# Gated mix of attention and a gated linear unit: two head groups' projections as 2x2 blocks with seven products, and five early head steps

## The chip, the cores and the metric

The kernel runs on one core of a Trainium2 chip. The metric is the time of one execution in microseconds; the figure given for a version is the median of its runs.

## The reference

One sequence of 2048 tokens, 512 wide. An attention with 32 heads of 16 and a gated linear unit with 1792 hidden channels are mixed by a gate per token:

```python
qkv = (x @ wqkv).reshape(B, S, 3, H, Dh)          # B, S, H, Dh = 1, 2048, 32, 16
p = softmax(einsum("bhqd,bhkd->bhqk", q, k) * Dh ** -0.5)
a = einsum("bhqk,bhkd->bhqd", p, v).reshape(B, S, D) @ wo
b = (sigmoid(x @ w_gate) * (x @ w_up)) @ w_down   # 512 -> 1792 -> 512
g = sigmoid((x * gate_w).sum(-1, keepdims=True))
out = g * a + (1 - g) * b
```

## The kernel before

**Precision.** Nearly every matrix product is made of high and low parts of its operands (f32r tiles): high by high, high by low and low by high, so each product of two 128-deep blocks is three matmuls. A `Sum` is such a product gathered in one PSUM bank; its matmuls are issued as halves of 64 rows (`Sum.half`, L161), the lower and the upper half of the array by turns.

**The steady loop.** Attention runs as 256 periods (`for k in range(NPER)`, L840), 16 for each of 16 pairs of heads. The string `STEADY` (L831) writes out the order of one period: the maxima's matmuls of a later stretch (L284, reduced by VectorE at L286), the score matmuls (L648, exponentials on ScalarE at L650), 12 filling halves, marked `d0` and `d1`, and then the 16 value matmuls (L781). The instructions of TensorE, VectorE, ScalarE and GpSimd (POOL) stay in the order written. SP, which issues nearly all DMAs, is not written in order: the scheduler places them, and SP then issues them strictly one after another. The last ten periods use `LAST`, with six halves.

**The filling.** The generator `filling()` hands out Sums. Jobs before, in order: the query and key projections of head groups 1, 2 and 3 (`qk`, 8 Sums of 24 halves each, periods k 0 to 47; group 0 is done ahead of the loop); then gate and up, whose 14 column blocks are taken in pairs as 2x2 blocks with seven products in place of eight, as Strassen and Winograd do: `far` (7 jobs, 4 products each), `side` (14 jobs of 4) and `chain` (14 jobs of 8), all of 12 halves, one product per period, up to k 243. In them x itself has to be replaced by sums and differences of its quarters (`mixed_x`, through `t_d` in memory); products are evicted by ScalarE (`out_of`), added by POOL (`plus`, L514) and stored to `gu_d` (L516). After them comes `heads`: for the first `EARLY` of eight steps u of the output projection, head groups 0 and 1 are summed in the loop (`first_heads_load`, `first_heads_split`) and kept in `hp_d`.

**Beside it.** The maxima of each half pair are split by POOL (`put_max`, L295; the cast at L311), stored in `max_d` (L304) and read back by four DMAs (L308) into the row of `qs` that the scores use. The logits of the gate are 16 VectorE instructions (L768) at k 78 to 125. The softmax denominators are turned into reciprocals by `denominators` (L756).

**The tail.** After the loop come 28 chunks of the down projection (L966, 24 matmuls each), and between them the eight steps `heads_out(u)`. A step below `EARLY` takes only head groups 2 and 3 and adds what `hp_d` holds:

```python
ks = range(2 if u < EARLY else 0, KT)
product(o, [((hl[0][:, n, cols], hl[1][:, n, cols]), (wohl[:, 0, k, :], wohl[:, 1, k, :]))
            for n, k in enumerate(ks)])
```

Each step has two output tiles; `product` is L148 in the profile.

## Time and profile before

| | before |
|---|---|
| median of 3 runs | 1695.69 us (1694.86 to 1696.26) |
| profiled execution | 1694.23 us, span 1692.5 us |
| TensorE busy | 1685.8 us, 100% of the span, granted clock 1.0 |
| VectorE, ScalarE, POOL busy | 1446.7, 1357.4, 880.7 us (85%, 80%, 52%) |
| chain that ended last | TensorE 96% |
| DMA | 223.51 MB, mean 132 GB/s |
| memory read, written | 131.33 MB, 89.92 MB |

The span runs from the first to the last instruction of the profiled execution; 1.73 us of that execution's time lie outside it. A line such as L308 is a line of the kernel before. PE is TensorE's matmuls, PEld its weight loads, DVE VectorE, ACT ScalarE, SPq the issue of a DMA on SP. The chain is the work that ended last, followed back from the last instruction to what released each piece. The profile is of one execution, and all durations below are its own.

### The profile page before, as it was taken

The page shows a single profiled execution, that of the slowest core. Times are in us where ns is not written, and L with a number is a line of the kernel's source. Part 1 is how long each engine was busy: PE and PEld are TensorE (multiplying, and loading weights), DVE is VectorE, ACT ScalarE, POOL GpSimd, SP SyncE. Part 2 cuts the span into 40 slices and gives each one's busy share as a digit, 9 for nine tenths or more (in the row PEclk, how much of TensorE's full clock was granted, in tenths as well). Part 3 has the DMA queues.
Part 4 walks back from the last instruction along what each step waited for, and adds up shares of the span by engine and source line. Part 5 has one row for each costly group of instructions (what it writes and reads, how often), then busy time and mean ns, then how long its engine had stood idle before and what let it go on. Part 6 is the DMA issues. An engine that isn't in the chain of part 4 may idle for free.

```text
span 1692.5 us, 34518 instructions
## 1 busy us (share of the span) xinstructions
PE 1685.8 (100%) x12509; PEld 1032.5 (61%) x12509; DVE 1446.7 (85%) x2333; ACT 1357.4 (80%) x2643; POOL 880.7 (52%) x862
## 2 busy tenths in 40 slices
PE   9999999999999999999999999999999999999999
PEld 7755555555555555555555555555555555568887
DVE  6988888888889989999888888889988888887643
ACT  4188888888898989888888989889898988984321
POOL 1033343447664555554666667676666667643110
PEclk9999999999999999999999999999999999999999
DMA  7412324254755352534625353535353434478762
GB/s 235 109 45 65 83 64 96 64 127 153 200 171 136 109 120 92 118 114 106 193 98 136 108 144 108 139 108 135 108 126 108 127 120 132 142 234 280 266 195 71
DMA packets 126922, 223.51 MB, mean 132 GB/s; under 512 B 23520, under 2 KB 33504, under 8 KB 123872
## 3 DMA queue, kind: packets, MB, share of 16 engines
q1 hardware_dynamic: 126752, 221.31, 44.9%
q8 instruction: 98, 1.61, 0.4%
q14 instruction: 72, 0.59, 0.1%
HBM read 131.33 MB, written 89.92 MB: 131 GB/s over the span
## 4 chain that ended last, share of the span: by engine, by line
PE 96%; DMA 1%; DVE 1%; POOL 1%; issue 0%; SPq 0%; ACT 0%; POOLq 0%; DVEq 0%
PE dn L161 30%; PE sm L781 27%; PE sm L284 12%; PE st L648 7%; PE sm L966 5%; PE sm L648 5%; PE st L284 2%; PE dn L966 2%; PE st L161 2%; PE st L966 2%; PE st L148 1%; PE st L612 1%; PE sm L148 1%; DVE stat L286 1%; DMA gul<-gu_d 1%
## 5 line engine op out<-in xcount | busy, mean ns | idle before, releaser
L286 DVE TENSOR_REDUCE stat<-sm 128x1 f32<-128x512 f32 x1310 | 848.5, 683 | 150.8 <-PE sm L648 129.6
L650 ACT ACTIVATE p<-st 128x512 f32<-128x512 f32 x1020 | 617.7, 652 | 1.4 <-PE st L648 0.8
L650 ACT ACTIVATE p<-sm 128x512 f32<-128x512 f32 x1026 | 608.8, 630 | 0.9 <-PE sm L648 0.9
L284 PE MATMUL sm<-ks,qs 48*128 48x512 f32 x1310 | 516.4, 435 | 0.3 <-DVE stat L286 0.3
L286 DVE TENSOR_REDUCE stat<-st 128x1 f32<-128x512 f32 x738 | 482.1, 681 | 0.1
L781 PE MATMUL sm<-p,v 128*17 128x512 f32 x4032 | 482.1, 595 | 0.0
L648 PE MATMUL sm<-qs,ks 64*128 64x512 f32 x1026 | 426.9, 419 | 0.3 <-DMA qs<-max_d 0.3
L648 PE MATMUL st<-qs,ks 64*128 64x512 f32 x1020 | 426.9, 419 | 0.2 <-DVE stat L286 0.2
L284 PEld LDWEIGHTS sm<-ks,qs 48*128 48x128 f32 x1310 | 233.9, 184 | 290.9 <-DVE stat L286 208.6
L798 POOL TENSOR_TENSOR sum<-sum,part 128x512 f32<-128x512 f32 x224 | 288.9, 1290 | 181.2 <-PE sm L648 169.1
L284 PE MATMUL st<-ks,qs 48*128 48x512 f32 x738 | 291.3, 395 | 0.0
L786 ACT ACTIVATE part<-sm 128x512 f32<-128x512 f32 x215 | 128.7, 599 | 133.0 <-issue 106.8
L781 PEld LDWEIGHTS sm<-p,v 128*17 128x17 f32 x4032 | 93.6, 96 | 227.2 <-issue 156.7
L648 PEld LDWEIGHTS st<-qs,ks 64*128 64x128 f32 x1020 | 187.7, 184 | 30.2 <-issue 3.4
L648 PEld LDWEIGHTS sm<-qs,ks 64*128 64x128 f32 x1026 | 189.1, 185 | 9.5 <-issue 4.3
L514 POOL TENSOR_TENSOR chain<-chain,chain 128x512 f32<-128x512 f32 x84 | 108.5, 1291 | 114.6 <-PE sm L648 112.1
L514 POOL TENSOR_TENSOR had<-chain,had 128x512 f32<-128x512 f32 x84 | 108.1, 1287 | 59.6 <-PE sm L648 43.0
L284 PEld LDWEIGHTS st<-ks,qs 48*128 48x128 f32 x738 | 137.8, 187 | 1.0 <-ACT v L631 0.3
L514 POOL TENSOR_TENSOR side<-side,side 128x512 f32<-128x512 f32 x28 | 36.1, 1291 | 92.7 <-PE sm L648 87.1
L576 ACT ACTIVATE chain<-dn 128x512 f32<-128x512 f32 x112 | 77.8, 694 | 0.0
L103 POOL TENSOR_TENSOR ol<-ot,oh 128x1024 fp32r<-128x1024 f32 (+1 forms) x8 | 16.4, 2054 | 101.9 <-ACT oh L100 101.9
L311 POOL CAST mhl<-mt 128x32 fp32r<-128x32 f32 x32 | 7.4, 233 | 102.7 <-DVE mt L292 102.7
(837 smaller groups left out, 3205.3 us busy)
## 6 DMA issues: line engine op xcount, KB each, us to landing
gul<-gu_d SPq DMA_DIRECT2D x56, 512.0 KB
had<-gu_d SPq DMA_DIRECT2D x84, 256.0 KB
gu_d<-had SPq DMA_DIRECT2D x84, 256.0 KB
gu_d<-side SPq DMA_DIRECT2D x56, 256.0 KB
qs<-q_d SPq DMA_DIRECT2D x90, 128.0 KB
ks<-k_d SPq DMA_DIRECT2D x90, 128.0 KB
pv_d<-sum SPq DMA_DIRECT2D x32, 256.0 KB
gu_d<-far SPq DMA_DIRECT2D x28, 256.0 KB
```

The source lines that it names most:

```text
L148: pe.matmul(o, a, b, start=(i == 0), stop=(i == len(ops) - 1))
L161: mm = pe.matmul(self.o, a[rows], b[rows], start=(self.n == 0), stop=(self.n == 2 * len(self.ops) - 1))
L284: pe.matmul(t, qs[r:r + KM, qt * P:(qt + 1) * P], ks[r:r + KM, g * 512:(g + 1) * 512], start=True, stop=True)
L286: dve.tensor_reduce(stat[half][:, b, qt % 8, g:g + 1], t, axis=AX.X, op=ALU.max)
L514: pool.tensor_tensor(to, u, w, ALU.add)
L576: leave = lambda e, o: act.activation(e, o, AF.Copy)
L648: pe.matmul(o, ks[r:r + KR, (kt + a) * P:(kt + a + 1) * P], qs[r:r + KR, q0:q0 + 512], start=True, stop=True)
L650: act.activation(pt[:, 2 * a + c, :], o, AF.Exp, scale=DH ** -0.5)
L781: pe.matmul(o[32 * c:32 * c + VW, :], v[:, 2 * k % 16 + a, h * VW:(h + 1) * VW], pts[c // 2][:, 2 * a + c % 2, :], start=(a == 0), stop=(a ...
L786: act.activation(e, o, AF.Copy)
L798: pool.tensor_tensor(s, s, e, ALU.add)
L966: pe.matmul(down[t], a, b, start=(f == 0 and m == 0), stop=(f == NF - 2 and m == 5))
```

## The change

`EARLY` becomes 5: steps u=3 and u=4, too, get the sums of head groups 0 and 1 in the loop, so `heads` has 10 Sums and not 6. The query and key projections of head groups 2 and 3 leave the `qk` jobs. They become an eighth `far` job and a `side` and a `chain` job each for queries (m=2) and keys (m=3), with groups 2 and 3 as the two column blocks. The jobs now run: `qk` 1 (k 0 to 15), eight `far` (16 to 47), `side` and `chain` of queries and keys (48 to 71), then `side` and `chain` of gate and up (72 to 239), then `heads`. The side job of the keys replaces quarters of x as that of gate and up does; for the side jobs that follow, `kept_x` stores these quarters beforehand in two more planes of `t_d` (8 DMAs of 512 KB), and the chain job of the keys fetches them back with `mixed_x`. The finished projections lie in `s_d` as f32; later, at k 75 to 122, they are fetched, split into high and low by POOL and stored to `q_d` and `k_d` (`split_load`, `split_sum`). The logits move three periods earlier, and the reciprocals of the first denominators are spread over twice as many pieces.

```diff
-EARLY = 3
+EARLY = 5
...
     pv_d = dram.tile([2, NPAIR, P, 512], F32, name="pv_d")
     hp_d = dram.tile([2 * EARLY, P, D], F32, name="hp_d")
-    t_d = dram.tile([3, 2, 2, 2, P, 512], F32, name="t_d")
+    t_d = dram.tile([5, 2, 2, 2, P, 512], F32, name="t_d")
+    s_d = dram.tile([2, 2, P, S], F32, name="s_d")
     max_d = dram.tile([2 * NPAIR, 4, 32, 2, 32], F32, name="max_d")
...
+    def kept_x(n, c, k0, cx):
+        cols = slice(cx * 512, (cx + 1) * 512)
+        for a, xs in enumerate((xh, xl)):
+            sp.dma_start(t_d[n, a, c].rearrange("k p s -> p k s"), xs[:, k0:k0 + 2, cols].bitcast(F32))
+
     def mixed_x(n, c, k0, cx):
 
         cols = slice(cx * 512, (cx + 1) * 512)
...
     def filling():
         pairs = [(m, i) for i in range(HF) for m in range(2)]
-        jobs = ([("qk", n) for n in range(1, D // P)] + [("far", i) for i in range(HF)]
-                + [("side", n) for n in pairs] + [("chain", n) for n in pairs] + [("heads", 0), ("down", 0)])
+        qk = [(2, 0), (3, 0)]
+        jobs = [("qk", 1)] + [("far", i) for i in range(HF + 1)]
+        for ns in (qk, pairs):
+            jobs += [("side", n) for n in ns] + [("chain", n) for n in ns]
+        jobs += [("heads", 0), ("down", 0)]
         gu_w = (w_gate, w_up)
+
+        def beside(m, i):
+            return i + HF if m < 2 else i + 1
 
         def raws(kind, n):
             if kind == "qk":
...
                 both = []
                 for m in range(2):
-                    sp.dma_start(raw[:, 2:], gu_w[m][n][:, 2:])
+                    sp.dma_start(raw[:, 2:], gu_w[m][n][:, 2:] if n < HF else wqk[2, 1, :, m])
                     both.append(raw)
                 return both
...
             if kind == "heads":
             m, i = n
+            if m >= 2:
+                return [raw_weights(wqk[f, :, :, m - 2].rearrange("b p k f -> p b k f"), [P, KT, P],
+                                    f"{kind}{m}_{f}") for f in (2, 3)]
             return [raw_cols(gu_w[m], i + a, f"{kind}{m}_{i + a}") for a in (0, HF)]
...
             return e
 
         def place(m, f, c):
-            return gu_d[m, f, :, c * 512:(c + 1) * 512]
+            to = gu_d[m, f] if m < 2 else s_d[m - 2, f]
+            return to[:, c * 512:(c + 1) * 512]
 
...
                     for c in range(2):
                         run = Sum(bankd(), quarter(ws[m], 2, c))
                         yield run
-                        sp.dma_start(place(m, n, c), out_of(run, f"far{m}{n}_{c}"))
+                        sp.dma_start(place(m, n, c) if n < HF else place(2 + m, 0, c), out_of(run, f"far{m}{n}_{c}"))
             elif kind == "side":
                 m, i = n
                 for c in range(2):
                     for a in range(2):
                         run = Sum(bankd(), quarter(ws[a], 2 * a, c + 2))
                         yield run
-                        if n == pairs[-1]:
+                        if n in (qk[-1], pairs[-1]):
                             mixed_x(1 + a, c, 2 * a, c + 2)
                         e = out_of(run, f"side{m}{i}_{c}{a}")
                         if a == 0:
                             first = e
-                            sp.dma_start(place(m, i + HF, c + 2), e)
+                            sp.dma_start(place(m, beside(m, i), c + 2), e)
                         else:
                             plus(e, e, first, place(m, i, c + 2))
             elif kind == "heads":
...
             else:
                 m, i = n
                 for c in range(2):
-                    to = [place(m, i, c), place(m, i, c + 2), place(m, i + HF, c + 2), place(m, i + HF, c)]
+                    i2 = beside(m, i)
+                    to = [place(m, i, c), place(m, i, c + 2), place(m, i2, c + 2), place(m, i2, c)]
...
                         run = Sum(bankd(), quarter(ws[a], k0, cx))
                         yield run
+                        if n == qk[-1] and a >= 2:
+                            mixed_x(1 + a, c, 2 * a - 4, c + 2)
                         e = out_of(run, f"chain{m}{i}_{c}{a}")
                         if a in (1, 2):
                             plus(e, e, first)
...
         def first_heads(u):
 
-            ks, q0 = slice(2 * (u // 2), 2 * (u // 2) + 2), (u % 2) * 256
+            ks, q0 = slice(u // 2 % 2 * 2, u // 2 % 2 * 2 + 2), (u % 2) * 256
             for at in (0, 2):
                 for xs in (xh, xl):
                     yield xs[:, ks, at * 512 + q0:at * 512 + q0 + 256]
...
                         mix_x(u // 2, u % 2)
                 if job == ("chain", pairs[-1]):
                     if at == 4:
-                        for u in range(EARLY):
+                        for u in range(4):
                             first_heads_load(u)
                     if at in (6, 7):
                         first_heads_split(at - 6)
-                if kind == "heads" and at == 2:
-                    first_heads_split(2)
+                if kind == "heads" and at in (2, 4, 6):
+                    if at == 2:
+                        first_heads_load(4)
+                    first_heads_split(at // 2 + 1)
                 if at == ask[kind][0]:
                     coming = raws(*nxt)
                 if at == ask[kind][1]:
...
             while end in later:
                 later.pop(0)[1]()
             ws = new
-            if kind == "far" and n == HF - 1:
+            if kind == "far" and n == HF:
                 flush(slow)
                 for c in range(2):
                     mixed_x(0, c, 2, c)
+                for c in range(2):
+                    kept_x(3, c, 0, c + 2)
+                    kept_x(4, c, 2, c + 2)
         wd.extend(ws)
...
 
+    split_in = {}
+
+    def split_load(r):
+        f, t, c = r // 8, r // 4 % 2, r % 4
+        e = split_in[r] = keep.tile([P, 2, 512], F32R, name=f"sq{r}", tag="ev", bufs=2)
+        sp.dma_start(e[:, 0, :].bitcast(F32), s_d[t, f, :, c * 512:(c + 1) * 512])
+
+    def split_sum(r):
+        f, t, c = r // 8, r // 4 % 2, r % 4
+        e = split_in.pop(r)
+
+        def store():
+            for a in range(2):
+                sp.dma_start((q_d, k_d)[t][a, (2 + f) * P:(3 + f) * P, c * 512:(c + 1) * 512],
+                             e[:, 1 - a, :].bitcast(F32))
+        split_later(e[:, 1, :], e[:, 0, :], e[:, 0, :].bitcast(F32), store)
+
...
 
-    dens = [denominators(0, 0, 32, 8), denominators(0, 32, 64, 2), denominators(1, 0, 64, 2)]
+    dens = [chain(denominators(0, 0, 32, 8), denominators(1, 0, 32, 8)), denominators(0, 32, 64, 2),
+            denominators(1, 32, 64, 2)]
...
-        if 78 <= k < 126:
-            t, r = divmod(k - 78, 6)
-            if r == 0:
+        if 75 <= k < 123:
+            t, r = divmod(k - 75, 6)
+            if r in (0, 3):
+                split_load(2 * t + r // 3)
+            if r in (1, 4):
+                split_sum(2 * t + r // 3)
+            if r == 1:
                 logit_load(2 * t)
             if r in (3, 4):
                 logits(2 * t, r - 3)
...
-        if 192 <= k < 202:
+        if 192 <= k < 212:
             next(dens[0], None)
         if k == NPER - 6:
             next(dens[1])
```

In the instruction order, names are tiles with the number of their buffer or of their use. The lines of the changed file are shifted: L149 is `product` (L148 before), L305 and L309 are the store and the loads of the maxima (L304 and L308), L378 and L379 the loads of heads and reciprocals (L372 and L373), L535 the store of an added sum (L516), L797 the store of split projections.

On TensorE, in the tail, step u=3 stands before chunk 15 of the down projection. `oh3` and `ol3` are the high and low parts of the heads, `wohl` the output weights, `sm0` and `st0` the two output tiles. Before, from the first matmul with `ol3` on:

```order
L148 MATMUL sm0_69<-wohl_18125,ol3_18599 128x512
L148 MATMUL sm0_69<-wohl_18125,oh3_18598 128x512 x2
L148 MATMUL sm0_69<-wohl_18125,ol3_18599 128x512
L148 MATMUL sm0_69<-wohl_18125,oh3_18598 128x512 x2
L148 MATMUL sm0_69<-wohl_18125,ol3_18599 128x512
L148 MATMUL sm0_69<-wohl_18125,oh3_18598 128x512 x2
L148 MATMUL sm0_69<-wohl_18125,ol3_18599 128x512
L148 MATMUL st0_65<-wohl_18125,oh3_18598 128x512 x2
L148 MATMUL st0_65<-wohl_18125,ol3_18599 128x512
```

After:

```order
L149 MATMUL sm0_69<-wohl_18348,ol3_18822 128x512
L149 MATMUL sm0_69<-wohl_18348,oh3_18821 128x512 x2
L149 MATMUL sm0_69<-wohl_18348,ol3_18822 128x512
L149 MATMUL st0_65<-wohl_18348,oh3_18821 128x512 x2
L149 MATMUL st0_65<-wohl_18348,ol3_18822 128x512
L149 MATMUL st0_65<-wohl_18348,oh3_18821 128x512 x2
L149 MATMUL st0_65<-wohl_18348,ol3_18822 128x512
L1012 MATMUL sm2_71<-wd2h_18243,hl15_18878 128x512
```

The first output tile goes from four groups of three matmuls to two, and the second likewise; the neighbouring chunks stay as they were.

On SP, near the end of the loop: `max_d<-mhl` is the store of the maxima of pair 15's first half, `qs<-max_d` their four loads, `xh` and `xl` the operands of an early head step, `gu_d<-had` the store of a sum of the chain. Before:

```order
L516 DMA gu_d<-had_00_16900 128x512
L304 DMA max_d<-mhl_0_17037 128x64
L308 DMA qs_101<-max_d 1x32x32 x4
L516 DMA gu_d<-had_00_16900 128x512
L372 DMA xh<-pv_d 128x1x256
L373 DMA xl<-rec_d 128x1x256
L372 DMA xh<-pv_d 128x1x256
L373 DMA xl<-rec_d 128x1x256
```

After:

```order
L535 DMA gu_d<-had_10_17127 128x512
L305 DMA max_d<-mhl_0_17280 128x64
L378 DMA xh<-pv_d 128x1x256
L379 DMA xl<-rec_d 128x1x256
L378 DMA xh<-pv_d 128x1x256
L379 DMA xl<-rec_d 128x1x256
L309 DMA qs_102<-max_d 1x32x32 x4
L535 DMA gu_d<-had_10_17127 128x512
```

Four loads of an early step (u=4) now stand between the store of the maxima and their four loads, where nothing stood.

On SP in the side jobs of gate and up, the maxima of pair 7's first half; `sq` is a tile with a split projection, `side` a sum of a side job. Before:

```order
L478 DMA gu_d<-side_00_8268 128x512
L107 DMA side_12r<-in_w_gate_dram 128x512
L304 DMA max_d<-mhl_0_8343 128x64
L308 DMA qs_101<-max_d 1x32x32 x4
L516 DMA gu_d<-side_01_8341 128x512
```

After:

```order
L789 DMA sq_8615<-s_d 128x512
L108 DMA side_12r<-in_w_up_dram 128x512
L305 DMA max_d<-mhl_0_8529 128x64
L797 DMA q_d<-sq_8400 128x512 x2
L309 DMA qs_102<-max_d 1x32x32 x4
L535 DMA gu_d<-side_01_8527 128x512
```

Two stores of a split projection now stand between the maxima's store and their loads; each follows POOL's split.

## The prediction

> **What bounds the kernel now.** I read the page's busy shares and its chain first.
>
> ```profile
> span 1692.5 us, 34518 instructions
> PE 1685.8 (100%) x12509; PEld 1032.5 (61%) x12509; DVE 1446.7 (85%) x2333; ACT 1357.4 (80%) x2643; POOL 880.7 (52%) x862
> PE 96%; DMA 1%; DVE 1%; POOL 1%; issue 0%; SPq 0%; ACT 0%; POOLq 0%; DVEq 0%
> ```
>
> TensorE is busy all the time and is 96% of the chain that ends last. So this is a question of how many matmuls are left, and of whether the changed work around them ever makes TensorE wait. An average cannot say that for a stage, so the second view is the table of windows, cut at the ends of the filling's jobs: in order the query and key job of group 1; groups 2 and 3; the far jobs; the side jobs; the chain jobs; the last periods; the tail. The columns are busy time and instructions of each engine, the granted clock, the DMA share and GB/s.
>
> ```profile
> core 0: us, PE busy (x) PEld busy (x) DVE busy (x) ACT busy (x) POOL busy (x), PEclk, DMA share, GB/s
> 88.90:172.60 83.70, 83.70 (x662) 48.49 (x660) 73.63 (x125) 71.16 (x143) 34.53 (x35) 1.00 0.20 57
> 172.60:351.40 178.80, 178.80 (x1410) 103.48 (x1408) 157.62 (x265) 152.42 (x305) 73.86 (x76) 1.00 0.31 76
> 351.40:507.90 156.50, 156.50 (x1234) 90.62 (x1232) 137.87 (x231) 140.29 (x282) 101.03 (x111) 1.00 0.58 172
> 507.90:821.50 313.60, 313.60 (x2470) 181.76 (x2470) 285.61 (x495) 280.55 (x561) 165.20 (x188) 1.00 0.46 122
> 821.50:1453.80 632.30, 631.81 (x4977) 365.55 (x4976) 561.81 (x942) 567.45 (x1135) 428.81 (x395) 1.00 0.43 124
> 1453.80:1497.50 43.70, 43.35 (x329) 19.81 (x328) 35.44 (x52) 43.14 (x90) 22.19 (x21) 1.00 0.36 120
> 1497.50:1692.50 195.00, 190.89 (x847) 155.72 (x845) 121.97 (x110) 70.60 (x77) 42.56 (x20) 1.00 0.65 213
> ```
>
> In every job the pace is the same: 178.80/1410 = 0.1268 us for a matmul record in the query and key window, 156.50/1234 = 0.1268 in the far window, 0.127 in the side and chain windows, at clock 1.00 throughout. A period with 12 filling halves takes 5.58 us whether the job is light (POOL 41% busy, DMA 0.31) or heavy (POOL 68%, DMA 0.43; VectorE and ScalarE at 89 and 90%). So a change of job kind costs nothing by itself as long as each period has its 12 halves.
>
> **The change, part by part.** *Projections.* Groups 2 and 3 took 16 Sums of 24 halves: 2 x 16 periods. Now one far, two side and two chain jobs have 28 products of 12 halves, 28 periods of one Sum each. Four periods' filling (48 halves, the work of 24 full matmuls) becomes free. *Heads.* The partial heads' sums grow from 6 to 10 Sums of 12 halves, 48 halves more. The two cancel: every period of the loop still has its 12 halves, the number of periods is fixed by the scores at 256, and so the loop becomes neither shorter nor longer. What is saved lies only in the tail: for steps u=3 and u=4, half of the four head groups is now summed in the loop, and each of their four output tiles takes 6 matmuls where 12 stood. From the chain in the tail, one piece for each output tile:
>
> ```profile
> 1590.73 2.72 PE sm L148 x12
> 1593.45 2.72 PE st L148 x12
> 1612.49 2.72 PE st L148 x12
> 1615.21 2.72 PE sm L148 x12
> ```
>
> The first two are step 3, the others step 4. Each piece of 12 matmuls at 0.227 us (2.72/12) becomes one of 6. All four are links of the chain, back to back with their neighbours: 4 x 6 x 0.2267 = **5.44 us saved**.
>
> *What goes the other way.* The new jobs bring more work for the other engines, at these durations:
>
> ```profile
> L576 ACT ACTIVATE chain<-dn 128x512 f32<-128x512 f32 x112 | 77.8, 694 | 0.0
> L514 POOL TENSOR_TENSOR chain<-chain,chain 128x512 f32<-128x512 f32 x84 | 108.5, 1291 | 114.6 <-PE sm L648 112.1
> L756 DVE RECIPROCAL den<-den x12: 498/530/1750, 1169.7 to 1539.9; 32x64 f32<-32x64 f32 x8, 32x256 f32<-32x256 f32 x2, 64x256 f32<-64x256 f32 x2
> ```
>
> Instead of 16 evictions there are 28 and 4 for the heads: 16 x 0.694 = 11 us more on ScalarE. POOL gets 28 more adds of 1.291 us: 36 us. VectorE gets eight reciprocals of 0.53 us: 4 us. I cost all of these at nothing, because the chain and side windows above, which have this mix in every period, run at the same 5.58 us; the cover is VectorE's 0.62 us per period ((632.30 - 561.81)/113 periods) and ScalarE's 0.57. If the cover were gone for one instruction, its excess over about 0.6 us would be lost. The 16 splits are moved from the groups' own periods (k 16 to 47) to k 75 to 122, so they now run beside the gate's logits and the side adds; each adds a cast and a subtraction to POOL. Their stores and the loads that feed them go past SP's other issues. VectorE gets four more adds in the tail, 0.7 us each, where it is busy 63% (121.97/195.00): nothing.
>
> *Where a wait can appear: SP.* Every eight periods the maxima go to memory and come back by four loads, which the scores wait for. SP works in order, so a transfer that waits for POOL and stands between the store and those loads holds the loads. This happens once in the program before, with a store of a sum between:
>
> ```profile
> 834.95 0.21 POOL L311 CAST mhl<-mt 128x32 fp32r<-128x32 f32 x1 [1.46 <-DVE mt L292]
> 836.69 1.29 POOL L514 TENSOR_TENSOR chain<-chain,chain 128x512 f32<-128x512 f32 x1 [1.19 <-PE sm L648]
> 838.06 1.28 POOL L514 TENSOR_TENSOR had<-chain,had 128x512 f32<-128x512 f32 x1
> 839.37 0.32 SPq L516 DMA_DIRECT2D gu_d<-had  x1
> 839.78 2.78 SPq L308 DMA_DIRECT2D qs<-max_d  x4
> 842.60 0.47 PE L648 MATMUL st<-qs,ks 64*128 64x512 f32 x1 [0.21 <-DVE stat L286]
> ```
>
> ```profile
> 838.31:844.40 6.09, 5.88 (x46) 3.27 (x44) 5.39 (x10) 5.25 (x11) 5.81 (x7) 1.00 0.22 65
> 844.40:849.98 5.58, 5.58 (x45) 3.26 (x44) 4.36 (x8) 4.87 (x11) 5.22 (x6) 1.00 0.51 171
> ```
>
> ```profile
> 880.78 0.32 SPq L304 DMA_DIRECT2D max_d<-mhl  x1
> 882.23 2.76 SPq L308 DMA_DIRECT2D qs<-max_d  x4
> ```
>
> The store waited until POOL's second add ended at 839.34, the loads followed, and the period took 6.09 us instead of 5.58 (the rows of windows): **0.51 us lost**. Eight periods later the loads start 1.45 us after the store of the maxima (880.78 to 882.23), and nothing is lost. After the change the order has such a neighbour in three further places. At the maxima of the first half of pair 15 (k 237) four loads of step 4's operands stand between. The first must wait until POOL has finished its product in the same buffers (about 1.28 us, as for a 128x512 above), and issues of this kind take 0.6 us each:
>
> ```profile
> 1418.31 2.76 SPq L308 DMA_DIRECT2D qs<-max_d  x4
> 1421.17 0.39 SPq L516 DMA_DIRECT2D gu_d<-had  x1
> 1421.65 0.64 SPq L372 DMA_DIRECT2D xh<-pv_d  x1
> 1422.35 0.60 SPq L373 DMA_DIRECT2D xl<-rec_d  x1
> ```
>
> The bounds are 0.1 (they issue while the maxima's store travels, 1.45 us, and of their 2.4 about 1.0 is left, most of it within the usual slack) and 1.0 us. I take 0.3, by nearness to the 0.51 of one waiting store. At the maxima of pair 5's second half (k 85) and pair 7's first (k 109) two stores of split halves stand there. POOL's cast and subtraction end early, because the cast of the maxima is 0.21 us and POOL is free for 47% of the side window; bounds 0 and 0.5 each, I take 0.05 each. The longer chain of reciprocals may cost 0.1 as a second instruction of 0.53 us beside a logit or none: 0.1 (bounds 0 and 8 x 0.1).
>
> *Transfers.* The kept halves of x (4 MB, then 4 MB back) and the f32 sums are new. They go in large packets or small:
>
> ```profile
> 504.00:506.00 2.00, 2.00 (x18) 1.55 (x15) 1.30 (x4) 1.69 (x4) 0.00 (x0) 1.00 0.99 320
> 532.00:534.00 2.00, 2.00 (x20) 1.56 (x16) 1.37 (x3) 1.72 (x4) 0.00 (x0) 1.00 1.03 127
> ```
>
> The first is the mixed x as today (320 GB/s), the second a pair's head loads (127 GB/s). About k 46 to 48, 2 MB of mixed x and some 1.5 MB of pair 4's loads meet: 2.1/0.320 + 1.5/0.127 = 6.5 + 12 = 18.5 us, against the six periods (33.5 us) until the scores need them. That is nothing, with 15 us to spare; a miss would cost what exceeds it.
>
> *Sum.* -5.44 + 0.3 + 0.1 + 0.1 = **-4.94 us**. The profiled execution took 1694.23, its span of 1692.5 and 1.73 around it, so it would take 1689.3. It lies 1.46 below the median of 1695.69; on the median's scale the forecast is 1695.69 - 4.94 = **1690.8 us**.
>
> **A rule that speaks against it.** The logits are the VectorE instructions with two operands in SBUF that the moved splits now run beside:
>
> ```profile
> L768 DVE CUSTOM_DVE_ANT_0 xn<-xn,gwb x16: 650/682/682, 537.4 to 778.4; 128x512 f32<-128x512 f32 x16
> ```
>
> POOL was 53% busy in that window (165.20/313.60), and not one of the 16 took over 682 ns: an instruction of POOL that had started first did not lengthen them. The Trainium skill, page "SBUF — State Buffer", section "Who interferes with whom", says that a VectorE instruction with two SBUF inputs contends with a GpSimd instruction that reads SBUF, and that the pair of ports is locked by whoever issues first. By that rule the added POOL work could hold up the logits; these 16 rows do not bear it out in that direction, and the rival below prices it from the rows.
>
> **Rivals.** *Partly given back.* Several small waits come together: 1.0 at the maxima of pair 15, 0.5 at each of the two others, 0.5 at the start where the first kept halves pass SP, some at the meeting of transfers. Then 2.5 us of the gain return: about 1693.2. For it: the order has these neighbours. Against: the one measured example costs 0.51.
>
> *The tail's feeds are late.* After the shift, the tail's TensorE arrives 5.44 us earlier at the last chunks, and the operands might not:
>
> ```profile
> 1639.73 0.75 DVE L934 SCALAR_TENSOR_TENSOR acc<-sm,g,acc 128x512 f32<-128x512 f32 x1 [0.61 <-PE sm L966]
> 1641.53 1.22 DVE L103 TENSOR_TENSOR hl<-gul,hl 128x1024 fp32r<-128x1024 f32 x1
> 1644.97 0.39 PE L966 MATMUL st<-wd2h,hl 128*128 128x512 f32 x1
> ```
>
> At chunk 22 the operand is ready at 1642.75, 2.22 us ahead of its matmul. If it did not move, 5.44 - 2.22 = 3.2 us would be lost: about 1693.5 (1695.69 - 2.22). Against: VectorE itself waited for TensorE just before (0.61), so it moves along.
>
> *The maxima come late everywhere (slower).* If SP's new traffic puts a waiting transfer ahead of the maxima's loads in all of the 14 maxima of the gate and up chain, the 2 of the new chain and the 2 named beside the side jobs, 18 x 0.51 - 0.51 (there today) = 8.7 us are lost: 1695.69 - 5.44 + 8.7 = 1698.9. It decides from 5.44/0.51 = 11 places on. For it: the example. Against: the new order shows three places more, not 17.
>
> *The logits wait for POOL (slower).* Each of 16 logits blocked by one add: 1.29 less VectorE's slack of 0.50 in the side window ((313.60 - 285.61)/56 periods) is 0.79, 16 x 0.79 = 12.6: 1702.9. Against: none of 16 was lengthened. Its rule is that of the Trainium skill cited above.
>
> *The change does not do what it says.* The order shows the two tail steps with half their matmuls and the same number of halves in every period; I leave this no chance of its own.
>
> **How the numbers follow.** Forecast 0.66 (1689.4 to 1691.6); partly given back 0.15 (1691.6 to 1695); late feeds 0.08; late maxima 0.08; logits 0.03. A measurement of this kernel can tell about 0.2%, 3.4 us, from no change, so faster means below 1692.3. That is all of the forecast, 0.06 of the second and 0.02 of the third: 0.74. The same: 0.09 + 0.06 = 0.15. Slower: 0.11. The range starts at the full 5.44 and the runs' spread of 0.8 (1694.86 against 1695.69): 1695.69 - 5.44 - 0.8 = 1689.4, and reaches to 1694.5, which takes in the late feeds and most of the second case.
>
> **What would show it.** In the profile after: windows of the loop at 5.58 us per period, and a tail shorter by 5.4 us with the pieces of steps 3 and 4 at 1.36 us; the loop's end at 1497.5 plus at most 1; a period of up to 5.9 about the maxima of pair 15 and none else new. Wrong: a loop that ends more than 2 us later, logits over 682 ns, or TensorE idle in the tail for operands.

## The result: slower by half a per cent, and the profile after

The changed kernel takes 1704.22 us (median of 4 runs, 1701.91 to 1707.11) beside 1695.28 for the kernel before (median of 4): a ratio of 1.0054, interval 1.0034 to 1.0075. The forecast was 1690.8, with a range to 1694.5. The profiled execution, the fastest of the four, took 1701.91 us, its span 1700.2; the account below is of that one.

The page of the changed kernel, the lines that answer to those of before:

```profile
span 1700.2 us, 34765 instructions
PE 1687.2 (99%) x12485; PEld 1029.9 (61%) x12485; DVE 1452.1 (85%) x2345; ACT 1365.3 (80%) x2659; POOL 934.9 (55%) x920
PE 94%; DMA 2%; DVE 2%; POOL 2%; issue 1%; SPq 0%; ACT 0%; POOLq 0%; DVEq 0%
```

TensorE has 24 matmul records fewer and a longer span; 2 points of its share of the chain went to DMA, VectorE and POOL. Where the time went is told by windows cut at the first value products, at those of k 239, at the loop's last period and at the end. The kernel before:

```profile
88.90:1425.23 1336.33, 1336.12 (x10518) 773.81 (x10516) 1190.89 (x2013) 1185.46 (x2367) 781.64 (x787) 1.00 0.42 116
1425.23:1501.00 75.77, 75.14 (x563) 38.25 (x561) 64.53 (x98) 73.03 (x150) 45.59 (x40) 1.00 0.51 168
1501.00:1692.50 191.50, 187.39 (x833) 153.37 (x832) 118.54 (x105) 67.11 (x72) 40.95 (x19) 1.00 0.65 213
```

The changed kernel:

```profile
89.42:1438.33 1348.91, 1343.01 (x10519) 774.74 (x10517) 1197.42 (x2023) 1194.84 (x2384) 847.42 (x852) 1.00 0.48 139
1438.33:1514.10 75.77, 74.85 (x561) 38.80 (x560) 62.32 (x96) 72.52 (x148) 35.90 (x32) 1.00 0.37 130
1514.10:1700.20 186.10, 181.96 (x809) 148.87 (x808) 119.69 (x109) 66.16 (x72) 39.04 (x19) 1.00 0.66 218
```

The tail is 5.40 us shorter, as forecast (5.44). The loop up to k 239 is 12.58 us longer with one matmul record more, and the start 0.52: together +7.7, the difference of the spans. Steps 3 and 4 now have pieces of 6 matmuls where they had 12, in the chain of the changed kernel's tail:

```profile
1603.86 1.36 PE sm L149 x6
1605.22 1.36 PE st L149 x6
1622.90 1.36 PE st L149 x6
1624.26 1.36 PE sm L149 x6
```

The loop lost most in three places. The windows are single periods, each ending at the value products of its k, and take 5.58 us when nothing is late (k 55 and 56, 134 and 135, 239 and 240):

```profile
391.55:400.00 8.45, 6.92 (x47) 3.92 (x45) 6.19 (x11) 5.68 (x11) 3.49 (x3) 0.86 0.50 166
400.00:406.09 6.09, 6.09 (x46) 3.31 (x45) 3.74 (x7) 4.63 (x10) 1.60 (x2) 0.91 0.92 283
838.88:845.99 7.11, 6.06 (x47) 3.25 (x45) 6.33 (x12) 5.28 (x11) 4.22 (x6) 1.00 0.56 178
845.99:852.23 6.24, 5.91 (x46) 3.27 (x45) 4.60 (x9) 5.07 (x11) 4.72 (x4) 1.00 0.17 55
1428.60:1438.33 9.73, 7.22 (x46) 4.24 (x45) 5.98 (x11) 5.52 (x11) 8.45 (x8) 0.85 0.59 167
1438.33:1444.09 5.76, 5.76 (x46) 3.24 (x45) 3.75 (x7) 4.63 (x10) 1.59 (x2) 0.96 0.93 321
```

That is 3.4, 2.2 (0.5 of it lost before, too) and 4.3 us; the rest, some 3 us, are periods that lost 0.1 to 0.7 (0.71 at k 78, where the maxima's end, a transposition and a logit follow each other on VectorE). Two of the three are the maxima's round trip. In the chain about k 55 and about k 239:

```profile
388.84 5.45 DMA max_d<-mhl
...
395.08 1.96 DMA qs<-max_d
...
397.17 0.47 PE st L672
...
1427.78 4.24 DMA max_d<-mhl
...
1432.81 2.25 DMA qs<-max_d
...
1435.20 0.64 PE st L672
```

The dots stand for pieces left out. The 32 KB store of the maxima took 5.45 and 4.24 us to land, where in the kernel before the loads that follow it started 2.30 and 1.45 us behind it. In the third place, at k 134, the chain and the timeline have:

```profile
836.42 5.07 DMA had<-gu_d
...
844.39 0.50 PE L162 MATMUL dn<-xh,ca(0, 0)h 64*128 64x512 f32 x1 [1.05 <-POOLq L173]
```

TensorE waited 1.05 us for an empty instruction of POOL, by which the second group of half products is let into a bank; POOL was behind because a part fetched for a chain's sum landed 5.07 us after its issue.

The granted clock is the other half of the price. In the first place, changed kernel:

```profile
396.00:398.00 2.00, 0.83 (x6) 0.81 (x8) 1.03 (x3) 0.39 (x2) 0.78 (x1) 0.92 0.04 6
398.00:400.00 2.00, 2.00 (x10) 1.20 (x8) 1.41 (x3) 1.42 (x3) 0.00 (x0) 0.50 0.89 260
400.00:402.00 2.00, 2.00 (x17) 0.44 (x16) 0.54 (x1) 1.08 (x2) 0.00 (x0) 0.73 0.76 113
```

After 1.53 us of idling (1526 ns up to 397.17) TensorE ran at 0.5 of its clock for about 3.4 us: all of the second window, and the shares of the first and third that give means of 0.92 and 0.73 (0.3 + 2 + 1.1). The place lost 3.4 us where the wait was 1.5. The Trainium skill, page "TensorE: Matmul & The Clock Gate", part 1, knows the half rate, but after an idle window of about 3.4 us; here less than half of that was enough, and the trace decides. It was not enough every time: the last section has the waits after which the clock stayed.

Theory T, with which I went on, blames transfers. The new order of jobs puts large transfers where the maxima's store, or a part for a chain's sum, must pass; TensorE idles for it, and the clock falls. Rivals: R, the number and order of issues on SP, as in the prediction; L, the added work of POOL, ScalarE and VectorE.

### The profile page after: what moved, and what is told of

It is laid out like the page before. It is cut to its first block, busy times and chain, and to the rows that moved or that the text cites. A ratio compares the mean times of both kernels' runs of the same rounds, so it can differ in the third digit from the quotient of the medians.

```text
span 1700.2 us, 34765 instructions
## 1 busy us (share of the span) xinstructions
PE 1687.2 (99%) x12485; PEld 1029.9 (61%) x12485; DVE 1452.1 (85%) x2345; ACT 1365.3 (80%) x2659; POOL 934.9 (55%) x920
## 4 chain that ended last, share of the span: by engine, by line
PE 94%; DMA 2%; DVE 2%; POOL 2%; issue 1%; SPq 0%; ACT 0%; POOLq 0%; DVEq 0%
PE dn L162 29%; PE sm L822 26%; PE sm L285 12%; PE st L672 7%; PE sm L1012 5%; PE sm L672 5%; PE st L285 2%; PE dn L1012 2%; PE st L162 2%; PE st L1012 2%; DVE stat L287 1%; PE st L636 1%; PE st L149 1%; PE sm L149 1%; DMA max_d<-mhl 1%
## 5 line engine op out<-in xcount | busy, mean ns | idle before, releaser
L533 POOL TENSOR_TENSOR chain<-chain,chain 128x512 f32<-128x512 f32 x96 | 123.8, 1290 | 134.2 <-PE sm L672 127.2
L533 POOL TENSOR_TENSOR had<-chain,had 128x512 f32<-128x512 f32 x96 | 123.6, 1287 | 75.5 <-PE sm L672 31.0
L533 POOL TENSOR_TENSOR side<-side,side 128x512 f32<-128x512 f32 x32 | 41.2, 1289 | 87.7 <-PE sm L672 87.7
L600 ACT ACTIVATE chain<-dn 128x512 f32<-128x512 f32 x128 | 88.7, 693 | 0.0
L104 POOL TENSOR_TENSOR ol<-ot,oh 128x512 fp32r<-128x512 f32 (+1 forms) x8 | 14.2, 1778 | 100.0 <-ACT oh L101 86.7
```

What stands on the lines that cost most here:

```text
L533: pool.tensor_tensor(to, u, w, ALU.add)
L600: leave = lambda e, o: act.activation(e, o, AF.Copy)
```

## The experiments

**Step 4's loads behind the maxima** (e1_u4_behind). The four loads that the prediction had named:

```diff
+            for load in both if behind is not None else ():
+                tc.add_manual_dep(load.ins, behind.ins.name, SYNC, reason="behind the rows of the maxima")
...
+            o_and_r(..., rows_in[15, 0] if u == 4 else None)
```

> The changed kernel, with one edit: the four loads of step u=4 wait until the maxima's rows of pair 15's first half have landed. Theory T (transfers): the maxima's store landed 4.24 us after its issue there, not 1.45, because those loads travel beside it; TensorE then idles 2.5 us and runs at a granted clock of 0.5 for some us more. The period of 9.73 us falls to 5.6 to 6.2, the whole to about 1698 to 1699 (1701.9 for the profiled execution, less 3.5 to 4.1). Theory R (issues on SP): the same, since the four issues are gone from between. Theory L (the added work of POOL, ScalarE and VectorE slows the loop in many small places): that period stays over 8 us and the time within 1 us of 1701.9.

1700.46 us (1697.62 to 1701.99; before 1694.06; ratio 1.0034, 1.0019 to 1.0048). In its trace k 239 and 240 still took 8.27 and 6.74 us, 3.9 over. So T and R were both wrong about which loads: the four were not the cause. L's expectation for this period (over 8 us) came true here, that for the time (within 1 us of 1701.9) did not; the run with fewer bytes in all early steps' loads, below, speaks to its reason. What SP waited for in that stretch of this run:

```profile
SPq L519 <- DMA gu_d<-had: 5.0, 1, 5.0
SPq L309 <- DMA max_d<-mhl: 3.3, 1, 3.3
```

SP stood 5.0 us (4.7 in the changed kernel's own trace) before a fetch that needed a store of the chain to have landed, with the maxima's store queued behind it. Ahead of that store went the 16 loads of steps 0 to 3, between 1406 and 1419 us of this trace. The Trainium skill, page "DMA: Bandwidth & Descriptors", section "Queues, rings and completion order", has all that SP issues in one row of rings, in which it starts in order; the 5.0 us fit that. In the kernel before they were 12 and came after the maxima of k 237 (1421.65 us, as the prediction's own row shows): with the filling 4 periods early, they now come ahead of it.

**Fewer bytes, same issues** (e2_few_bytes).

```diff
-        cols = slice(cx * 512, (cx + 1) * 512)
+        cols = slice(cx * 512, cx * 512 + (64 if few else 512))
...
+            w = 32 if few else 256
```

> The changed kernel with all its DMA issues in place, but fewer bytes in two places: the mixed quarters of x fetched in the last side job of the keys carry 64 of 512 columns, the four loads of step u=4 carry 32 of 256 columns (the rest isn't loaded, so the keys of two groups and step 4 are computed from other data). T: at k 55 the store of the maxima lands in under 3.5 us where it took 5.45, and the period of 8.45 us falls below 6.0; at k 239 the store lands in 2 to 3 us and the period of 9.73 falls by 1.5 to 4. About 1696 to 1699. R: the issues are as many, so both periods stay within 0.5 us of what they were, 1701 to 1702. L: the same as R.

1697.81 us (10 runs; ratio 1.0021, 1.0011 to 1.0030). The periods at k 55 and 239:

```profile
391.72:397.29 5.57, 5.57 (x46) 3.22 (x45) 4.84 (x9) 4.97 (x11) 3.49 (x3) 1.00 0.42 133
1424.74:1434.01 9.27, 7.33 (x45) 4.20 (x44) 5.97 (x11) 5.53 (x11) 8.45 (x8) 0.81 0.47 132
```

At k 55 the loss is gone with the bytes alone, with every issue in its place: T, not R or L. At k 239 the loss stayed (3.7 us, and 1.6 in the next period; 4.2 and 0.2 in the changed kernel), where T had expected 1.5 to 4 us less: as in the run before, step 4's bytes are not it. The total lies in T's range although this part of T's reason failed.

**The blocks alone** (e3_blocks_only): `EARLY = 3` in the changed kernel.

> The changed kernel with three early steps, not five: the blocks alone. 48 halves fewer in the loop (48 x 0.127 = 6.1 us less), the tail as before. T: the stall at k 55 stays (8.4 us period), that at k 239 is gone since step 4's loads are gone; the loop ends 6.1 us earlier less about 7 us of stalls that are not those of k 239, so 1695 to 1698. R: the same. L: all periods of the new side and chain jobs stay slow, also 1695 to 1698, but the loss is spread and not at k 55.

1705.69 us (ratio 1.0074, 1.0054 to 1.0094); all three theories missed it. k 239 has no loss, as expected, but the 48 halves fewer did not shorten the loop: its last 16 periods took 77.62 us and not 75.77. The tail took 194.83 us and not the 191.50 of before; why it is 3.3 us longer stays open. A half product of the filling has no price of its own there; the run with blank periods below shows it directly.

**A priced byte ahead of the maxima** (e4_probe), in the kernel before.

```diff
+JUNK = {18: 1, 20: 2, 22: 3, 24: 4, 26: 5, 28: 6}
...
+            ahead = [sp.dma_start(junk_d[j]..., (xh, xl)[j % 2][:, 0:2, ...]) for j in range(JUNK.get(2 * p + i, 0))]
             put = sp.dma_start(d.rearrange("k r a j -> (k r) a j"), hl.bitcast(F32))
```

> The kernel before, with stores of 512 KB of x to an unused place issued just ahead of the store of the maxima: 1 at k 141, 2 at k 157, 3 at k 173, 4 at k 189, 5 at k 205 and 6 at k 221. It prices a byte ahead of the maxima. T: each 512 KB at 320 GB/s delays the landing by 1.6 us; one costs nothing or little, two some 0.5 us, three to six make TensorE idle 2 to 7 us, and from an idle of about 1.5 us on the granted clock falls to 0.5 for about 4 us, which adds some 2 us to each; 20 to 30 us in all. R: only the issues count, 0.42 us each: six of them 2.5 us, at most 1 us lost at each place, under 4 us in all. L: nothing.

1723.96 us in one run, 30 more than before. The periods after 2, 3, 4, 5 and 6 stores:

```profile
972.93:979.28 6.35, 5.88 (x46) 3.31 (x44) 5.65 (x10) 5.24 (x11) 6.07 (x7) 1.00 0.42 126
1062.98:1072.00 9.02, 7.17 (x46) 4.22 (x44) 6.19 (x11) 5.70 (x11) 8.64 (x10) 0.84 0.59 185
1155.89:1168.26 12.37, 7.34 (x46) 4.24 (x44) 6.19 (x11) 5.70 (x11) 9.28 (x10) 0.85 0.61 190
1253.65:1265.55 11.90, 7.35 (x47) 4.22 (x45) 6.20 (x11) 5.70 (x11) 9.30 (x10) 0.78 0.75 238
1350.06:1363.49 13.43, 7.35 (x47) 4.21 (x45) 6.19 (x11) 5.69 (x11) 9.27 (x10) 0.71 0.80 254
```

One costs nothing; two cost 0.8 us; from three on (1.5 MB) TensorE idles 1.9 to 6.1 us and with the following period loses 3.7 to 9.1: 1.8 to 3.3 us beyond the idling, with the clock at 0.71 to 0.85 in those periods. T's sizes hold, in one run; R's (under 4 us in all) do not.

**The same transfers in another order** (f1_behind). The second pair of mixed quarters waits for the maxima's rows at k 53, and of the early steps' loads only those of u=0 and 1 stay ahead.

```diff
+                            if n == qk[-1] and (a, c) == (1, 0):
+                                later.append((0, lambda: mixed_x(2, 0, 2, 2, rows_in[3, 1])))
...
-                        for u in range(4):
+                        for u in range(2):
                             first_heads_load(u)
...
+                if kind == "heads" and at == 0:
+                    for u in (2, 3):
+                        first_heads_load(u, rows_in[15, 0])
```

> The changed kernel with the same transfers in another order: in the last side job of the keys the second pair of mixed quarters of x waits for the maxima's rows at k 53, and of the early steps' loads only those of u=0 and 1 stay ahead of the maxima at k 237, those of u=2, 3 and 4 wait for their rows. Theory T, as the first four runs leave it: at k 239 it is not step 4's four loads but the 16 loads of steps 0 to 3 (127 GB/s, some 16 us), now ahead of the maxima, that make a store of the chain land after 5.0 us and hold SP for it, then make the maxima's store land late. T expects: the period at k 55 under 6.0 (8.45 in the changed kernel), the two at k 239 and 240 together 11.2 to 12.5 (15.5), the whole 1696 to 1698. Theory R (the number of issues): as many issues, so 1700 or more. Theory L (added work of the engines): both periods as they were, 1702 to 1704.

1694.87 us (10 runs) beside 1694.39 before; ratio 1.0002, 0.9992 to 1.0011. The loss against the kernel before is gone, further than T had expected (1696 to 1698); the loop up to k 239 is still 6.4 us longer than before, and the shorter tail pays for it. Periods k 55, 134, 135 and 239:

```profile
391.97:397.55 5.58, 5.58 (x46) 3.24 (x44) 4.87 (x9) 5.00 (x11) 3.53 (x3) 1.00 0.54 160
835.75:843.28 7.53, 6.12 (x47) 3.27 (x45) 6.42 (x13) 5.37 (x11) 4.27 (x6) 0.99 0.52 168
843.28:850.41 7.13, 7.13 (x45) 3.35 (x44) 3.86 (x8) 4.74 (x11) 3.96 (x4) 0.78 0.15 48
1426.56:1432.14 5.58, 5.58 (x45) 3.23 (x44) 4.67 (x9) 4.84 (x11) 5.44 (x6) 1.00 0.21 68
```

Two places are free of loss with as much work, as many issues and as many bytes. That goes against L, and against R as a count of issues. R as the order of issues it does not exclude, since the edit changes the order; the runs with fewer bytes, whose order is that of the changed kernel, do. The third place, untouched, stayed.

**Later jobs where they were** (f2_blanks). Three early steps, and four empty slots ahead of the side jobs of gate and up.

```diff
+            if job == ("side", pairs[0]):
+                for _ in range(4):
+                    yield BLANK
```

> Three early steps and the blocks, as the run of the blocks alone, and four periods with an empty filling at k 72 to 75, so that every later job starts at the period at which it starts in the kernel before. T: the loss at k 134 and 135 (2.2 to 2.4 us) falls to 0.7 or less, that at k 239 stays away, that at k 55 stays (1.8 to 3.6); the four blank periods are 0.3 to 0.6 us shorter each; the tail as before; 1695 to 1698. L: the new jobs cost the same wherever they stand, so the loss at k 134 stays and only the blanks gain: 1702 to 1704.

1703.74 us (ratio 1.0056), not 1695 to 1698. The loss at k 134 is gone and 135 lost 0.94, where T wanted 0.7 or less for the two together: the place depends on where the jobs stand, as T says. The time is within L's range, but L's reasons (k 134 stays, the blanks gain) both failed. The blank periods did not shrink at all. One of the four:

```profile
494.57:500.15 5.58, 5.58 (x33) 2.90 (x32) 4.88 (x9) 4.58 (x10) 0.00 (x0) 1.00 1.05 317
```

33 matmul records, not 45 to 48, in the same 5.58 us. TensorE's share of busy time reads 100% either way. The half products run beside the others at no cost, so the blocks gain only what is put into the slots that they free; what keeps a blank period at 5.58 us stays open. The tail of this version, without the two early steps, gains nothing: it took 193.9 us, 2.4 more than before, and this, too, stays open.

**Logits a period earlier** (f3_behind_logits): `k - 74` for `k - 75`, on f1_behind.

> The run with the reordered transfers, and the logits with the splits one period earlier (k 74 to 121). The first of two logits then no longer stands in the period right after the maxima's end. T says nothing of it; by the trace VectorE's maxima, the transposition and a logit meet at k 78 and 102 and cost 0.71 and 0.45 us: those fall to 0.25 or less each, 0.5 to 0.9 us under the run with the reordered transfers alone. L (POOL and VectorE in each other's way all along the side jobs): the two losses move to other periods and the time is the same.

1695.16 us, ratio 1.0005 (0.9995 to 1.0015). The losses at k 78 and 102 fell to 0.15 and 0.13 as expected, but the time did not follow: in this trace 4.0 us were lost at k 211 and 212, by a fetched part that landed 6.7 us after its issue beside a pair's loads, and 1.3 at k 195. Its runs lay between 1693.80 and 1699.85, so a gain of 0.9 us can't be seen. Inconclusive for the time.

**Few bytes in all early steps' loads** (f4_fewer_bytes): the run with few bytes, with `few` for every u.

> The run with few bytes, and now all the early steps' loads carry 32 of 256 columns (early steps computed from other data): the SP order and the number of issues stay. T: the chain's store before the maxima at k 237 lands in under 3 us where it took 5.0, the maxima's store in 1.5 to 2.5, and the periods at k 239 and 240 take 11.2 to 12.0 together (15.5 in the changed kernel, 16.4 with few bytes in step 4 alone). 1693 to 1695. R: 1697 to 1698, as with few bytes in step 4 alone.

1695.11 us (10 runs, ratio 1.0005), 0.1 over T's range. k 239 and 240:

```profile
1425.84:1431.42 5.58, 5.58 (x45) 3.24 (x44) 4.66 (x9) 4.84 (x11) 5.44 (x6) 1.00 0.25 64
1431.42:1437.01 5.59, 5.59 (x47) 3.26 (x45) 4.89 (x9) 5.02 (x11) 4.68 (x5) 1.00 0.88 250
```

That is the same cure as by order, by bytes alone, with the order and the work of the changed kernel. The run with few bytes in step 4 alone kept the loss, so the transfers of the 16 other loads are the cause at k 239.

**Weights behind the maxima** (g2_weights) and **parts fetched earlier** (g3_ahead).

```diff
+                                    rows_in[3, 0] if (kind, m) == ("side", 3) else None
...
+                        if (c, a) == (0, 3):
+                            nextpart = keep.tile([P, 2, 512], F32, name=f"had{m}{i}_10", tag="ev", bufs=2)
...
+                    for load in ahead:
+                        tc.add_manual_dep(store.ins, load.ins.name, NOSYNC, reason="loads ahead of a store")
```

> The run with reordered transfers and logits one period earlier, and the weights of the keys' side job behind the maxima's rows at k 45. T: 0.75 us is lost at k 47 and 48 because the maxima's store lands after 3.8 us beside those weights; it lands in under 3 us and at most 0.4 us is lost. About 0.4 us under 1695.2. L: no change.

> The same, and in each chain job the parts to which the fifth and sixth product are added are fetched one product earlier and ahead of the store of the fourth sum. T: at k 134 POOL waits for such a part (issued at 833 to 836, landed 5 us later), and with it the empty instruction of POOL that lets the next half products begin; fetched some 2 us earlier, TensorE's wait of 1.0 to 1.4 us there falls under 0.4, the loss at k 134 and 135 from 2.2 to 3.5 us to 1.0 or less. 1692 to 1693.5, the first version under the kernel before (1694.4). R (SP's order is what it is): the wait at k 134 as before, 1695. L: no change.

1703.13 and 1702.90 us: both missed. Moved behind the maxima's rows, the weights came late themselves, in g2_weights:

```profile
366.39 0.72 POOL L445 TENSOR_TENSOR side_3r<-side_3r 128x256 f32<-128x256 f32 x1 [8.71 <-DMA side_3r<-in_wqk_dram]
369.17 0.79 PE L162 MATMUL dn<-xh,side(2, 0)h 64*128 64x512 f32 x1 [6.45 <-POOLq L173]
```

The loss at k 47 went, as expected, and 9.6 us were lost at k 49 and 50. In g3_ahead the loss at k 134 and 135 fell to 0.46 us, as T expected of the parts.

**The parts alone** (h1_ahead on f3_behind_logits, h2_ahead on f1_behind).

> The run with reordered transfers and logits one period earlier (1695.2), and the parts of the chain's sums fetched one product earlier, as in the run before, but the weights of the keys' side job again where they were. T: the loss at k 49 (9.0 to 9.6 us, weights that came late) is gone, 0.8 us at k 47 and 48 is back, the loss at k 134 and 135 stays under 0.7 (2.3 in the run with the logits alone). 1692.5 to 1694, under the kernel before (1694.5) by 0.5 to 2. R and L: 1695.

> The run with reordered transfers alone (1694.9), and the parts of the chain's sums fetched one product earlier. T: the loss at k 134 and 135 (3.5 us in its trace, 2.2 in others) under 0.7, the 0.7 and 0.45 at k 78 and 102 stay. 1692.5 to 1694. R and L: 1695.

1693.43 us (11 runs, 1691.95 to 1699.15; ratio 1.0001, 0.9992 to 1.0010) and 1694.88 (11 runs, ratio 1.0002), beside 1694.16: the first within T's range of 1692.5 to 1694, the second not. k 134 and 135 in h1_ahead:

```profile
834.78:840.36 5.58, 5.58 (x46) 3.24 (x44) 5.30 (x11) 5.01 (x11) 4.46 (x6) 1.00 0.38 137
840.36:846.41 6.05, 5.89 (x46) 3.28 (x44) 5.34 (x10) 5.24 (x11) 4.34 (x4) 1.00 0.13 46
```

The wait at k 134 is cured, here and in h2_ahead (0.46 us lost at the two periods), so the late part was its cause. The profiled executions, with spans of 1691.7 and 1690.5 us, lie under the 1692.5 of before, but the medians cannot be told from it: no version here is shown to be faster.

**The changed kernel again, twice** (i1_after_again, i2_after_again), since its runs lay near 1702 and near 1706.5.

> The changed kernel once more, unchanged. At 1702: losses at k 55 to 57, 134 and 135, 239 and 240 as in its first trace. At 1706: V expects 4 to 5 us more at these three places together, with as many stretches at a granted clock under 1 but longer ones; W expects a further place with over 2 us lost and an idle TensorE that waits for POOL.

> The changed kernel a third time, unchanged, with the same expectations as the run before: V 4 to 5 us more at the three known places, W a further place.

V puts the difference into the three known places, W into a further one. The two runs took 1699.93 and 1705.27 us. Between the two traces the loop differs by 5.3 us: 2.3 at the three known places (V), and 2.5 at two that only the slower has (W), k 67 and k 211 (6.70 and 7.03 us). TensorE's waits for POOL's empty instruction came to 3.6 us in 4 in the slower trace, to 1.8 us in 2 in the faster. So neither alone holds, by one trace each. That the spread of the other runs is of the same kind, late landings that reach a place or not and a clock that falls or not, is likely but not shown; why a given transfer lands late in one run and not in another stays open.

## Why the prediction was wrong, step by step

- *The pace of a period does not depend on the job:* held in the main. Most periods took 5.58 us, with side, chain or no filling; those of the logits and of a reciprocal below took more. The condition given, 12 halves in each period, has no part in it: without them it is the same 5.58 us. So the opening reading, that the time is a question of how many matmuls are left, failed for the filling's halves.
- *Slots cancel, so the gain lies in the tail, 5.44 us:* held, 5.40; the late feeds of the rival did not come. What counts there are the slots, as the prediction has it, and not the time of the halves.
- *ScalarE, POOL and VectorE's extra work costs nothing:* held at the two largest losses, which f1_behind and f4_fewer_bytes took away with the work unchanged. It did not hold for the logits and the reciprocals, below.
- *Where a wait can appear: SP,* 0.3 + 0.1: the step that failed. The place k 239 was right, the loads and the bound (1.0 us) were not: 4.3 us measured. (At k 85 and 109, for which 0.1 stood in the sum, 0.14 and 0.13 us were lost.) I counted issues between a store and its loads, and did not follow where the 16 earlier loads went, although the row at 1421.65 shows them behind the maxima's loads before. The price of 0.51 us was that of a short wait; it holds neither a landing of 4 to 5 us nor the fall of the clock.
- *Transfers: "nothing, with 15 us to spare":* failed. It asked only whether the moved bytes arrive in time for their own users, not who queues behind them. At k 55 the maxima's store did, for 3.4 us. At k 134 a part of a chain's sum came late: 2.2 us, 0.5 of them lost before, too, and the sum had no term for it.
- *The 0.1 for the reciprocals* was 0.5 (k 206, where one follows the maxima's end and the transposition on VectorE). *The logits* were a term that the sum lacked: the periods of the side jobs that meet them lost 2.2 us, 1.0 before.
- *The logits wait for POOL:* shown for two of 16, at a small price, and the prediction's reading of the rows before was wrong. "Logits over 682 ns" was one of its signs of being wrong, and it came:

```profile
L809 DVE CUSTOM_DVE_ANT_0 xn<-xn,gwb x16: 680/682/1112, 526.0 to 767.0; 128x512 f32<-128x512 f32 x16
665.45 1.27 POOL L839 TENSOR_TENSOR sum<-sum,part 128x512 f32<-128x512 f32 x1
666.16 1.11 DVE L809 CUSTOM_DVE_ANT_0 xn<-xn,gwb 128x512 f32<-128x512 f32 x1
```

  The median is that of before, but one logit took 1112 ns and another 820. These two alone began well inside an add of POOL with two operands in SBUF (`sum<-sum,part`), 0.6 and 0.3 us before its end, and both ended 0.55 us after it. This is the rule of the Trainium skill, page "SBUF — State Buffer", section "Who interferes with whom", that such a VectorE instruction contends with a GpSimd instruction that reads SBUF, and that issue order decides who blocks; the trace agrees. Of the 16 before, none began with more than 0.03 us of such an add left, so those rows could not speak against the rule. In eight of the nine other runs with the logits at the same periods both are long (1104 to 1124 and 818 to 835 ns), in the ninth one of them; a period earlier (f3_behind_logits, h1_ahead), where none began inside an add, none took over 693. The two cost VectorE 0.6 us together, not the 12.6 of the rival.
- *The slower rival, late maxima* (0.08): the right resource, with another mechanism. It wanted 18 places at 0.51 us; there were two at 3.4 and 4.3.

## What to carry to other kernels

When a change moves a job in time, list the transfers that move with it and ask of each what small round trip now queues behind it; a transfer that arrives in time for its own user can still make another late. Check by an experiment whether work on the resource that reads 100% busy has a price: take it out of a few periods and see whether they shrink. And price a long stall of TensorE above its length.

## What the runs showed of the hardware

- All twelve waits of TensorE of 1.85 to 6.45 us in the loops of the kept traces were followed by a granted clock under 1, and their period and the next lost 1.8 to 3.3 us more than the wait. Between 1.2 and 1.75 us it went either way: the clock fell after 1.21 (e3_blocks_only, k 247), 1.41 (f1_behind), 1.50 (i2_after_again), 1.53 (the changed kernel) and 1.60 us (g3_ahead); it stayed after 1.22 and 1.52 (e3_blocks_only), 1.30 and 1.50 (e1_u4_behind), 1.74 (f2_blanks) and 1.47 us (i1_after_again). The last is at k 55, as above:

```profile
398.00:400.00 2.00, 2.00 (x22) 0.61 (x19) 1.54 (x3) 1.95 (x4) 0.00 (x0) 1.00 0.86 230
```

- 1 MB of stores ahead of the maxima's 32 KB store cost 0.8 us, 1.5 MB cost 3.7 (e4_probe, one run).
- Half-array matmuls beside others were free: 33 matmul records in a blank period of f2_blanks or 45 and more in a full one, 5.58 us both.
- A VectorE instruction with two operands in SBUF that began while POOL added two such operands took 0.14 and 0.43 us longer (two of two in the changed kernel).
